# Unread matmuls taken out, two scalings moved from VectorE to GpSimd, and token lists by fp32r products, in a delta-rule attention and mixture-of-experts kernel

## The chip, the cores and the metric

The kernel runs on one core of a Trainium2 chip. The metric is the time of one execution on the device, in microseconds, as the median of several executions. Engines are called by their short names in the profile: PE is the matrix engine, DVE is VectorE, ACT is ScalarE, POOL is GpSimd, and SP is the engine whose queue issues most of the DMA transfers.

## The reference

Two stages follow each other. The first is a linear attention with a delta rule, for 4 batches of 8 heads, 768 positions and 48 channels. The second routes each of the 3072 tokens to one of 8 experts.

```python
for t in range(S):                       # 768 positions
    kt, vt, bt = (k_n[:, :, t], v[:, :, t], beta[:, :, t, None])
    y[:, :, t] = np.einsum('bhd,bhde->bhe', q[:, :, t], state)
    v_old = np.einsum('bhde,bhd->bhe', state, kt)
    state = state + bt[..., None] * np.einsum('bhd,bhe->bhde', kt, vt - v_old)
...
x = y.transpose(0, 2, 1, 3).reshape(3072, 384)
logits = x @ w_gate + modality_bias[modality_id]
e_idx = np.argmax(logits, axis=1)
gate_w = softmax(logits)[np.arange(N), e_idx]
for e in range(8):
    mask = e_idx == e
    out[mask] = gate_w[mask, None] * (np.maximum(x[mask] @ w1[e], 0) @ w2[e])
```

## The kernel before

**The attention.** The 768 positions are cut into 12 chunks of 64, and each chunk into two halves, which gives 24 steps with the index `i`, where `c = i//2` is the chunk. In every step PE makes a handful of small float32 products: `ks` (keys with the state, L416), `y1` and `r` (the chunk's triangular inverse, L380 and L388), `z` (the inverse with the right-hand side, L422), `ds` (the state's update, L428), `qs` and `pz` (the outputs, L436 and L439). DVE and ACT copy the results out of PSUM; `rh` (L418) forms the right-hand side on DVE from the values `vv` and `ks`. Before `rh`, the values of each step are scaled in place by the task `vs` (L393), which multiplies a 128x384 tile. By default `vs` runs on GpSimd; a mark at its place in the order sends it to DVE.

The triangular inverses of the chunks come from a forward substitution for all heads at once (L332 and L333, alternately a multiply and a subtract), in three jobs `J` of four chunks each. Their results go through DRAM: `rd` and `re` store them (L351, L354), and `rl` loads them back in another layout (L371, L374). Loads of keys (`kq`, L153) and values (`kv`, L158), these stores and loads, and the store of outputs (`xd`, L441) all go through SP's one queue, in order.

**The order.** All of the attention's work, the first half of the router and the beginning of the first expert's work are 948 numbered tasks. `ORDER` (L28 to L50) is a list of their numbers, written out by hand; a letter behind a number chooses another engine (`d` is DVE, `g` is GpSimd). `emit` (L495) issues the tasks in this order, and each engine keeps to it strictly. `FILL` (L52) is a second list: `k:n` puts `n` products of the identity with itself (128x128x128, float32) ahead of task `k` (L499). They add into columns of a PSUM bank that nothing reads. Tasks that the prediction names: 557 and 620 are the router products `lg0` and `lg1`, 579 is `z5`, 590 `ks6`, 107 the product `pg4`, 615 `pz7`, 764 `ks17`, 744 the transposes `xt15`, 909 the transposes `xp3` of gathered rows, 866 the transposes `xt23` of the last output tile, 408 and 414 `vs8` and `vs9`, both halves of chunk 4.

**The router and the lists.** Each output tile is transposed (`xt`, L570) and multiplied by the gate weights (`lg`, L575). `part_a` does the ranking for the first 16 tiles, and makes the lists for two units of 512 tokens; it is cut into tasks `pa0` to `pa16` of the order. `part_b` does it for all 24 tiles, after the attention, beside the first expert's work; there and in all later work the order is that of the framework's scheduler. A unit's list says for each of its places which token stands there and with which gate. `lists` (L674) makes it by products: `A` is a one-hot matrix of a token's rank within 128 (L633), and `B` holds, for every block of 128 places, the token's number and its gate where the token belongs to that block, else zero (L690 to L692). Four tiles at a time make a group; the sum over all tiles of `A` transposed with `B` (L698) is the list. In list a, `B` has 2 x 8 columns, in list b 2 x 17.

**The experts.** Each unit gathers its rows (L797, GpSimd's indirect DMA), transposes them (L800), and splits rows and weights into a high and a low part in fp32r, so that three single-pass products give float32 precision (L837 for the first layer, L892 for the second). The result is scaled by the gate (L895) and scattered to the output (L896).

Of the kernel before, what the change touches and what calls it, by code (L numbers as in the profile page):

```python
# [35 lines left out]
68 70 392d 81 396 387d 398 298 537 82 399 299g 546 538 84 400 539 271 548d 86 547 83 85 300 540 311 401 549 541 560 301g 545 562 10 11 552 561 550 302g 551d 564 553d 575 566 303g  # L36
565d 554 555 577 563 556 576 567 304 557 568 305 570 569 306 579 307 558 571 312 572 573 580 578 574 12 313 397 308 309 402 590 581d 359 314 96 585 360 310 582 586 361 592 587 403
13 315 593 583 591 362 99 594 97 595 596d 101 107 98 100 316g 559 584d 317g 600 110 605 318g 601 108 597 602 409 606 111 319g 112 608 598 607 603 599d 14 609 109 320 623 611 588 610
321 589 615 322 604 612 616 414d 618 614 626 323 619 613 620 15 408d 324 621 617 404 625 325g 405 415 624 406 622 638 407 326 627 410 426 639 629 118 411 421 628d 327g 640 412 121 633
119 413 630 634 122 420d 120 123 416 635 328 631 636 427 641 417 637 329 642 632 418 644 330 643 16 653 419 648 655 422 331 649 645 423 433 651 647 654 424 332 652 656 646 17 425  # L40
657 333 668 650 659 129 658 334g 669 670 663 132 660 664 130 428 133 665 661 335 131 134 671 439 429 672 662 432d 430 336 674 673 686 431 18 438 678 687 675 688 679 337 434 680 676
689 19 435 338 681 677 445 436 339 690 437 701 340 692 440 691 702 666 341g 441 696 703 667 442 682 697d 342 698 705 443 450d 704 707 343 693 706 20 444d 711 694 344 708 695 345 683
# [59 lines left out]
class Attention:  # L102
# [35 lines left out]
    def bank(s,n,t): return s.ps.tile([128,512],F32,name=n,tag=t)  # L138

    def plan(s):  # L140
# [318 lines left out]
            add(f"xd{i}","SP",.45,lambda i=i: xd(i),[f"xo{i}"],mb=.2)  # L459
            s.router.tasks(plan,s,i)  # L460

        tp=lambda NH: s.S[0][:,384:384+2*NH].rearrange("q (a b) -> q a b",a=2)
        end=plan.chain("pa",lambda dry: (R.mute() if dry else R).part_a(*(((Mute(),)*3,)+(Mute(),)*4 if dry else (s.places,s.sea,s.prt(),s.mo,tp))),["lt3","y1_17"],prio=900)
        x={}
        def xe(): x["S"]=s.X.slot_of(*s.first)
# [64 lines left out]
class Router:  # L530


    def __init__(s,tc,pc,wg,mod,bias,tok,ident):
        nc=tc.nc; s.tc=tc; s.nc=nc; s.ident=ident; NT=24
        def T(sh,nm,dt=F32): return pc.tile(sh,dt,name=nm)
        s.wg=T([128,3,32],"wg"); mi=T([128,NT,2],"modi",I32); s.tid=T([128,NT],"tid"); bb=T([128,2,8],"mbias")
        s.loads=((s.wg,wg.rearrange("(k p) e -> p k e",p=128)),(mi,mod.bitcast(I32).rearrange("q (t w) -> q t w",w=2)),(bb,bias.rearrange("(o m) e -> o m e",o=1).to_broadcast([128,2,8])),(s.tid,tok))
        s.mi,s.bb=mi,bb
        s.LT=T([128,NT,32],"LT"); s.xt,s.lg,s.le={},{},{}
        s.m=[T([128,NT],f"m{k}") for k in range(2)]; s.L=T([128,NT,8],"L"); s.bt=T([128,NT,8],"btok")  # L540
        G=nc.gpsimd
        s.tri=T([128,128],"tri"); ii=s.tri.bitcast(I32); G.iota(ii,pattern=[[1,128]],base=0,channel_multiplier=0)
        s.iot=T([128,128],"iotf"); G.tensor_copy(s.iot,ii); G.memset(s.tri,1.0)
        G.affine_select(out=s.tri,in_=s.tri,compare_op=ALU.is_gt,fill=0.0,base=0,pattern=[[1,128]],channel_multiplier=-1)
        s.ones=T([128,128],"ones"); G.memset(s.ones,1.0)
        s.keep=T([128,8,NT],"keep"); G.memset(s.keep,1.0); G.memset(s.keep[:,:,0],0.0)
        s.W=T([128,8,NT],"W"); G.memset(s.W,0.0)
        s.zero=T([128,8],"zero8"); G.memset(s.zero,0.0)
        s.em8=T([128,8],"em8"); G.tensor_scalar(s.em8,s.iot[:,0:8],-8.0,None,ALU.add)
        s.edge={512:T([128,6],"edge512"),256:T([128,12],"edge256"),128:T([128,1],"edge128")}  # L550
        G.tensor_scalar(s.edge[512],s.iot[:,1:7],512.0,None,ALU.mult); G.tensor_scalar(s.edge[256],s.iot[:,0:12],256.0,128.0,ALU.mult,ALU.add); G.memset(s.edge[128],0.0)
        s.lo=T([128,NT],"rlo",I32); s.OH=T([128,NT,8],"OH"); s.r=T([128,NT],"rank"); s.gt=T([128,NT],"gtok")
        s.F=T([128,8],"taken"); G.memset(s.F,0.0)

    def load(s,k): s.nc.sync.dma_start(*s.loads[k])
# [28 lines left out]

    def mute(s):
        d=copies.copy(s)
        for n in ("nc","slot","L","LT","bt","em8","ones","tri","W","keep","OH","r","lo","gt","iot","tid","zero","F","edge"): setattr(d,n,Mute())
        return d

    def rank(s,t0,t1,pw,bank):  # L590

        yield "DVE",1.4
        nc=s.nc; V=nc.vector; n=t1-t0; u=f"_{t0}"
        T=lambda sh,nm: pw.tile(sh,F32,name=nm+u,tag=nm,bufs=1)
        Z=s.slot(9 if t0 else 0,"rt"+u)
# [78 lines left out]
    def lists(s,u,t,pi,NH,ids,o0,out,pw,tp,k,zeroed):  # L674
# [2 lines left out]
        nc=s.nc; V=nc.vector; G=getattr(nc,C.lb_e)  # L677
        T=lambda sh,nm,dt=F32: pw.tile(sh,dt,name=nm+u,tag=nm,bufs=1)
        gate,gidx,sidx=(x[:,o0:o0+NH] for x in out)
        if u!="r": V.tensor_scalar(pi,pi,7,None,ALU.arith_shift_right)  # L680
        H=4; AB=[None,None]; ms=[]
        for h in range(0,t+H,H):
            if h<t:
                yield "DVE",.7+3*(.13+H*NH*1e-3)
                if h==0: AB,LB=(s.slot(k+n,f"l{n}"+u) for n in range(2))
                z=slice(512*(h//H%2),512*(h//H%2)+512); A=AB[:,z].rearrange("q (t c) -> q t c",t=H)
                s.onehot(A,h,H)
                B=LB[:,z][:,0:H*2*NH].rearrange("q (h b n) -> q h b n",h=H,b=2)
                bn=lambda a:a[:,h:h+H].unsqueeze(2).to_broadcast([128,H,NH])
                V.tensor_tensor(B[:,:,0],ids.unsqueeze(1).to_broadcast([128,H,NH]),bn(pi),ALU.is_equal)  # L690
                G.tensor_tensor(B[:,:,1],B[:,:,0],bn(s.gt),ALU.mult)
                V.tensor_tensor(B[:,:,0],B[:,:,0],bn(s.tid),ALU.mult)  # L692
                ms.append((h,A,B))
            if h or t==H:
                yield "PE",.5
                g,A,B=ms.pop(0)
                for i in range(H):
                    nc.tensor.matmul(tp.rearrange("q a b -> q (a b)"),A[:,i],B[:,i].rearrange("q a b -> q (a b)"),start=(not zeroed and g+i==0),stop=(zeroed or g+i==t-1),skip_group_check=zeroed)  # L698
        yield "DVE",2.0
        tk=T([128,NH],"tk"); V.tensor_copy(tk,tp[:,0])  # L700
        V.tensor_scalar(gidx,tk,-1.0,0.0,ALU.add,ALU.max)
        V.tensor_copy(gate,tp[:,1])
        a=T([128,NH],"ta",I32); b=T([128,NH],"tb",I32); c=T([128,NH],"tcc",I32); z=T([128,NH],"tz"); f=T([128,NH],"tf"); f2=T([128,NH],"tf2")
        V.tensor_scalar(a,gidx,8,6,ALU.arith_shift_right,ALU.logical_shift_left)
        V.tensor_scalar(b,gidx,63,None,ALU.bitwise_and)
# [26 lines left out]
    def part_b(s,out,sei,sei2,sei3,pw,bank):  # L732
# [255 lines left out]
```

## Time and profile before

| | |
|---|---|
| median of 3 runs | 499.58 us (498.87 to 504.86) |
| the profiled execution | 500.59 us, with a span of 498.9 us |
| mean granted clock of TensorE | 0.97 |
| busy: PE, DVE, ACT, POOL | 463.8, 324.0, 216.4, 118.4 us |
| DMA | 78.22 MB, 157 GB/s on the mean |
| attention, up to the last output tile | about 0 to 259 us |
| list a / list b on PE | 220.9 to 229.1 / 305.8 to 322.5 us |

A row of a timeline gives the start in us, the duration, the engine, the line, the operation with its output and inputs, the number of instructions run together, and in brackets how long the engine stood idle before it and which instruction ended that. A row of the chain gives start, duration and what ran. A row of a table of stretches gives the stretch, its length, the busy time and number of instructions of PE, PE's weight loads, DVE, ACT and POOL, then the granted clock as a share of full speed, the DMA engines' busy share and GB/s. One float32 matmul appears as two records of PE.

### The profile page before, as it was taken

What the parts mean: (1) busy time and instruction counts of PE and PEld (TensorE: products, weight loads), DVE (VectorE), ACT (ScalarE), POOL (GpSimd) and SP (SyncE); (2) the same over time, 40 slices, a digit from 0 to 9 for tenths busy, and PEclk for the clock granted to TensorE, in tenths of its full rate; (3) what the DMA queues carried; (4) which work ended last, traced back from release to release, by engine and by line L of the source; (5) the groups of instructions that cost most, each with busy time, mean ns of one, the idle gap of its engine ahead of it and who ended that gap; (6) DMA issues with size and microseconds to landing.
All of it is one profiled execution on the core that took longest, in us unless ns stands there. A gap on an engine that the chain in (4) does not pass through costs nothing.

```text
span 498.9 us, 15679 instructions
## 1 busy us (share of the span) xinstructions
PE 463.8 (93%) x6589; PEld 423.9 (85%) x6589; DVE 324.0 (65%) x676; ACT 216.4 (43%) x444; POOL 118.4 (24%) x154
## 2 busy tenths in 40 slices
PE   6889999999798979999799999997999999999994
PEld 6779999988698867898678898986898898899993
DVE  2698668889678774787677896525345355347751
ACT  2513467555456752653445433214234334226540
POOL 9011421446032103113311030065022131021111
PEclk8689999999989999998999999998999999999999
DMA  8759105387767877466645544145236326227730
GB/s 268 237 127 251 52 10 148 96 277 236 185 151 209 227 271 196 80 195 188 193 133 157 170 157 129 55 152 206 81 110 204 97 88 197 64 78 239 226 110 22
DMA packets 81328, 78.22 MB, mean 157 GB/s; under 512 B 48041, under 2 KB 71607, under 8 KB 79968
## 3 DMA queue, kind: packets, MB, share of 16 engines
q1 hardware_dynamic: 78048, 67.49, 45.8%
q0 software_dynamic: 3200, 9.64, 5.6%
q8 instruction: 54, 0.88, 0.7%
q14 instruction: 26, 0.21, 0.1%
HBM read 62.42 MB, written 14.88 MB: 155 GB/s over the span
## 4 chain that ended last, share of the span: by engine, by line
PE 71%; DMA 9%; DVE 9%; ACT 4%; issue 4%; SPq 1%; another core or an unknown queue 1%; POOL 0%; POOLq 0%; DVEq 0%; ACTq 0%
PE hpb L837 10%; PE opb L892 9%; PE opa L892 5%; PE gp L181 4%; PE lv L388 3%; PE hpc L837 3%; PE hpa L837 3%; PE opc L892 3%; DMA vv<-in_kv_dram 3%; PE S L499 3%; DMA kqr<-in_kq_dram 2%; PE y L439 2%; PE z L422 2%; PE S L428 2%; PE S L483 2%
## 5 line engine op out<-in xcount | busy, mean ns | idle before, releaser
L892 PE MATMUL opb<-w2hb,h 128*128 128x384 f32 x192 | 52.8, 340 | 0.5 <-DVE oob L895 0.5
L843 DVE SCALAR_TENSOR_TENSOR h<-hpb,h 128x512 fp32r<-128x512 f32 x24 | 16.6, 691 | 43.3 <-ACT h L841 43.3
L837 PE MATMUL hpb<-xh,w1xb 128*128 128x512 f32 x144 | 41.9, 403 | 0.0
L892 PEld LDWEIGHTS opb<-w2hb,h 128*128 128x128 f32 x192 | 34.8, 188 | 1.8 <-DVE oob L895 1.0
L841 ACT ACTIVATE h<-hpb 128x512 fp32r<-128x512 f32 x24 | 14.4, 598 | 50.5 <-PE hpb L837 50.5
L892 PE MATMUL opa<-w2ha,h 128*128 128x384 f32 x128 | 34.3, 342 | 0.6 <-DVE ooa L895 0.6
L892 PE MATMUL opb<-w2lb,h 128*128 128x384 f32 x96 | 32.5, 338 | 0.0
L837 PEld LDWEIGHTS hpb<-xh,w1xb 128*128 128x128 f32 x144 | 27.6, 194 | 4.7
L418 DVE TENSOR_TENSOR RHS<-vv,ks 64x384 f32<-64x384 f32 x44 | 24.2, 550 | 7.4 <-remote 3.7
L332 POOL TENSOR_TENSOR tmx<-T,A 128x456 f32<-128x456 f32 (+10 forms) x20 | 14.2, 710 | 58.1 <-DVE T L333 57.5
L25 ACT COPY Sb<-S 48x192 f32<-48x192 f32 x68 | 21.3, 313 | 13.6 <-PE S L428 7.2
L499 PE MATMUL S<-ident 128*128 128x128 f32 x154 | 25.6, 307 | 1.5 <-DVE Sb L26 0.5
L25 ACT COPY ZT<-z 64x384 f32<-64x384 f32 x36 | 17.0, 472 | 22.6 <-PE z L422 19.6
L499 PEld LDWEIGHTS S<-ident 128*128 128x128 f32 x154 | 21.4, 211 | 3.3 <-issue 0.7
L797 POOL DMA_INDIRECT xgb<-xd,gidxb x12 | 12.5, 1046 | 49.2 <-DVE tf2b L709 24.2
L896 POOL DMA_INDIRECT out_dram<-oob,sidxb x12 | 12.5, 1040 | 49.2 <-DVE oob L895 28.6
L892 PEld LDWEIGHTS opa<-w2ha,h 128*128 128x128 f32 x128 | 23.0, 188 | 1.3 <-DVE ooa L895 0.8
L181 PE MATMUL gp<-kqr 48*64 48x64 f32 x896 | 18.7, 236 | 5.6 <-DMA kqr<-in_kq_dram 3.7
L332 DVE TENSOR_TENSOR tmx<-T,A 128x396 f32<-128x396 f32 (+14 forms) x40 | 21.6, 540 | 2.6 <-POOL T L333 1.8
L422 PE MATMUL z<-RHS,R 128*64 128x96 f32 x384 | 22.0, 256 | 1.2 <-PE gp L181 0.5
L181 PEld LDWEIGHTS gp<-kqr 48*64 48x64 f32 x896 | 16.5, 149 | 7.5 <-DMA kqr<-in_kq_dram 4.3
L416 PE MATMUL ks<-Sb,kqr 112*64 112x96 f32 x352 | 20.3, 250 | 2.5 <-DVE RHS L418 2.2
(348 smaller groups left out, 1195.0 us busy)
## 6 DMA issues: line engine op xcount, KB each, us to landing
kqr<-in_kq_dram SPq DMA_DIRECT2D x10, 1024.0 KB, 5.9
ke<-in_kq_dram SPq DMA_DIRECT2D x10, 512.0 KB, 9.1
vv<-in_kv_dram SPq DMA_DIRECT2D x12, 384.0 KB, 6.5
xd<-xo SPq DMA_DIRECT2D x24, 192.0 KB, 6.3
w1rb<-in_moe_w_dram SPq DMA_DIRECT2D x12, 384.0 KB
w2rb<-in_moe_w_dram SPq DMA_DIRECT2D x12, 384.0 KB, 3.1
kk<-in_kv_dram SPq DMA_DIRECT2D x11, 384.0 KB, 5.0
w1ra<-in_moe_w_dram SPq DMA_DIRECT2D x8, 384.0 KB, 4.8
```

The lines of the kernel that those rows point to most:

```text
L25: if n=="scalar": nc.scalar.copy(o,i)
L181: s.I[f"g{c}"]=mm(t[k][o:o+64,64*(4*g+j):64*(4*g+j)+64],l,s.KQ[c][u:u+48,g,x,1] if a else l,start=True,stop=True)
L332: E[s.e].tensor_tensor(o,T[:,:,lo:lo+na,c:c+1].to_broadcast([128,n,na,nb]),X[:,:,c:c+1,c+1:32].to_broadcast([128,n,na,nb]),ALU.mult)
L388: for h in range(2): x=2*j+h; mm(o[0:64,x],s.YS[i%2][:,x],R[:,x,32:64] if i>7 else w0(s.Wn[i//4],i)[:,4*h+j],start=True,stop=True)
L416: for p in range(2): mm(s.ks[i][64*p:64*p+64,:,j,:],s.KQ[c][:,g,4*p+j,0],hc(s.Sb[g][:,4*p+j,:]),start=True,stop=True)
L418: c,g=divmod(i,2); b=64*p; V.tensor_tensor(s.RHS[g][b:b+64,:,48*p:48*p+48].rearrange("q (h j) c -> q h j c",h=2),s.KV[c,1][b:b+64,g],s.ks[ ...
L422: for h in range(2): mm(s.z[i][64*h:64*h+64,:,j,:],s.R[i%4][:,2*j+h,:],hc(s.RHS[i%2][:,4*h+j,:]),start=True,stop=True)
L499: for _ in range(fill.get(t["k"],0)): s.nc.tensor.matmul(s.S[1][:,384:512],s.ident,s.ident,start=False,stop=True,skip_group_check=True)
L837: if n in ks: mm=s.nc.tensor.matmul(hp[:,v,:],w[:,k,fs],x[:,k,0:T],start=(n==0),stop=(n==8))
L841: if k==0: s.nc.scalar.activation(hh,hp,AF.Relu)
L843: s.nc.vector.scalar_tensor_tensor(hl,hp,0.0,hh.bitcast(F32),ALU.max,ALU.subtract)
L892: mm=nc.tensor.matmul(op,h[:,f%nf,ts_],w[:,f%2,:],start=(n==0),stop=(n==23)); n+=1
```

## The change

- Twenty-one of the 77 unread products go: all of those ahead of tasks 107, 557, 579, 590, 615, 620, 744, 866 and 909, and two of the three ahead of 764.
- Tasks 408 and 414 lose their mark `d`, and so run on GpSimd, at the same places of the order.
- The lists use fp32r operands. The gate is split into a high part (rounded to fp32r) and the rest, and `B` gets four columns for each block instead of two: the token's number, the high gate, the low gate, and the mask they are made from, whose product is not read. The two gate sums are added behind the product. The list for the units beyond the planned ones, `r`, takes two tiles for a group instead of four.

```diff
 ORDER="""...
-... 612 616 414d 618 614 626 323 619 613 620 15 408d 324 621 ...
+... 612 616 414 618 614 626 323 619 613 620 15 408 324 621 ...
...
-FILL="""107:3 114:10 147:6 226:2 248:3 262:2 351:2 353:8 365:2 395:3 406:4 448:2 557:1 579:2 590:4 615:1 620:1 744:1 753:2 764:3 866:5 909:1 913:3 916:2 917:1 924:3"""
+FILL="""114:10 147:6 226:2 248:3 262:2 351:2 353:8 365:2 395:3 406:4 448:2 753:2 764:1 913:3 916:2 917:1 924:3"""
...
+    def split(s,t0,t1):
+        V=s.nc.vector; g,h,l=(x[:,t0:t1] for x in (s.gt,s.gh,s.gl))
+        V.tensor_copy(h.bitcast(F32R),g); V.tensor_tensor(l,g,h,ALU.subtract)
...
+        if u=="a": s.split(0,t)
+        elif u=="b": s.split(0,t)
         if u!="r": V.tensor_scalar(pi,pi,7,None,ALU.arith_shift_right)
-        H=4; AB=[None,None]; ms=[]
+        H=2 if u=="r" else 4; AB=[None,None]; ms=[]
...
-                if h==0: AB,LB=(s.slot(k+n,f"l{n}"+u) for n in range(2))
+                if h==0: AB,LB=(s.slot(k+n,f"l{n}"+u,F32R) for n in range(2))
...
-                B=LB[:,z][:,0:H*2*NH].rearrange("q (h b n) -> q h b n",h=H,b=2)
+                B=LB[:,z][:,0:H*4*NH].rearrange("q (h b n) -> q h b n",h=H,b=4)
                 bn=lambda a:a[:,h:h+H].unsqueeze(2).to_broadcast([128,H,NH])
-                V.tensor_tensor(B[:,:,0],ids.unsqueeze(1).to_broadcast([128,H,NH]),bn(pi),ALU.is_equal)
-                G.tensor_tensor(B[:,:,1],B[:,:,0],bn(s.gt),ALU.mult)
-                V.tensor_tensor(B[:,:,0],B[:,:,0],bn(s.tid),ALU.mult)
+                V.tensor_tensor(B[:,:,3],ids.unsqueeze(1).to_broadcast([128,H,NH]),bn(pi),ALU.is_equal)
+                for x,y in ((1,s.gh),(2,s.gl),(0,s.tid)): G.tensor_tensor(B[:,:,x],B[:,:,3].bitcast(F32),bn(y),ALU.mult)
...
-        V.tensor_copy(gate,tp[:,1])
+        V.tensor_copy(gate,tp[:,1]); V.tensor_tensor(gate,gate,tp[:,2],ALU.add)
```

`G` in `lists` is the engine that the class `C` names as `lb_e`, VectorE before and after.

More of the change, by code (lines that the diff above doesn't have):

```diff
@@ L38 @@
 13 315 593 583 591 362 99 594 97 595 596d 101 107 98 100 316g 559 584d 317g 600 110 605 318g 601 108 597 602 409 606 111 319g 112 608 598 607 603 599d 14 609 109 320 623 611 588 610
-321 589 615 322 604 612 616 414d 618 614 626 323 619 613 620 15 408d 324 621 617 404 625 325g 405 415 624 406 622 638 407 326 627 410 426 639 629 118 411 421 628d 327g 640 412 121 633
+321 589 615 322 604 612 616 414 618 614 626 323 619 613 620 15 408 324 621 617 404 625 325g 405 415 624 406 622 638 407 326 627 410 426 639 629 118 411 421 628d 327g 640 412 121 633
 119 413 630 634 122 420d 120 123 416 635 328 631 636 427 641 417 637 329 642 632 418 644 330 643 16 653 419 648 655 422 331 649 645 423 433 651 647 654 424 332 652 656 646 17 425
@@ L460, in plan @@
             s.router.tasks(plan,s,i)
-        tp=lambda NH: s.S[0][:,384:384+2*NH].rearrange("q (a b) -> q a b",a=2)
+        tp=lambda NH: s.S[0][:,384:384+4*NH].rearrange("q (a b) -> q a b",a=4)
         end=plan.chain("pa",lambda dry: (R.mute() if dry else R).part_a(*(((Mute(),)*3,)+(Mute(),)*4 if dry else (s.places,s.sea,s.prt(),s.mo,tp))),["lt3","y1_17"],prio=900)
@@ L551, in __init__ @@
         G.tensor_scalar(s.edge[512],s.iot[:,1:7],512.0,None,ALU.mult); G.tensor_scalar(s.edge[256],s.iot[:,0:12],256.0,128.0,ALU.mult,ALU.add); G.memset(s.edge[128],0.0)
-        s.lo=T([128,NT],"rlo",I32); s.OH=T([128,NT,8],"OH"); s.r=T([128,NT],"rank"); s.gt=T([128,NT],"gtok")
+        s.lo=T([128,NT],"rlo",I32); s.OH=T([128,NT,8],"OH"); s.r=T([128,NT],"rank"); s.gt,s.gh,s.gl=(T([128,NT],n) for n in ("gtok","ghi","glo"))
         s.F=T([128,8],"taken"); G.memset(s.F,0.0)
@@ L586, in mute @@
         d=copies.copy(s)
-        for n in ("nc","slot","L","LT","bt","em8","ones","tri","W","keep","OH","r","lo","gt","iot","tid","zero","F","edge"): setattr(d,n,Mute())
+        for n in ("nc","slot","L","LT","bt","em8","ones","tri","W","keep","OH","r","lo","gt","iot","tid","gh","gl","zero","F","edge"): setattr(d,n,Mute())
         return d
@@ L679, in lists @@
         gate,gidx,sidx=(x[:,o0:o0+NH] for x in out)
+        if u=="a": s.split(0,t)
+        elif u=="b": s.split(0,t)
         if u!="r": V.tensor_scalar(pi,pi,7,None,ALU.arith_shift_right)
-        H=4; AB=[None,None]; ms=[]
+        H=2 if u=="r" else 4; AB=[None,None]; ms=[]
         for h in range(0,t+H,H):
             if h<t:
-                yield "DVE",.7+3*(.13+H*NH*1e-3)
-                if h==0: AB,LB=(s.slot(k+n,f"l{n}"+u) for n in range(2))
-                z=slice(512*(h//H%2),512*(h//H%2)+512); A=AB[:,z].rearrange("q (t c) -> q t c",t=H)
+                yield "DVE",.7+4*(.13+H*NH*1e-3)
+                if h==0: AB,LB=(s.slot(k+n,f"l{n}"+u,F32R) for n in range(2))
+                z=slice(512*(h//H%2),512*(h//H%2)+512); A=AB[:,z][:,0:128*H].rearrange("q (t c) -> q t c",t=H)
                 s.onehot(A,h,H)
-                B=LB[:,z][:,0:H*2*NH].rearrange("q (h b n) -> q h b n",h=H,b=2)
+                B=LB[:,z][:,0:H*4*NH].rearrange("q (h b n) -> q h b n",h=H,b=4)
                 bn=lambda a:a[:,h:h+H].unsqueeze(2).to_broadcast([128,H,NH])
-                V.tensor_tensor(B[:,:,0],ids.unsqueeze(1).to_broadcast([128,H,NH]),bn(pi),ALU.is_equal)
-                G.tensor_tensor(B[:,:,1],B[:,:,0],bn(s.gt),ALU.mult)
-                V.tensor_tensor(B[:,:,0],B[:,:,0],bn(s.tid),ALU.mult)
+                V.tensor_tensor(B[:,:,3],ids.unsqueeze(1).to_broadcast([128,H,NH]),bn(pi),ALU.is_equal)
+                for x,y in ((1,s.gh),(2,s.gl),(0,s.tid)): G.tensor_tensor(B[:,:,x],B[:,:,3].bitcast(F32),bn(y),ALU.mult)
                 ms.append((h,A,B))
@@ L755, in part_b @@
         s.experts("b",hi,C.SB,sei,pw)
-        s.pib=pi; s.rest=lambda bank: s.lists("r",24,pi,m+NE-s.nm,s.ids[:,s.nm:],s.nm,out,pw,bank[:,0:2*(m+NE-s.nm)].rearrange("q (a b) -> q a b",a=2),6,False)
-        yield from s.lists("b",24,pi,s.nm,s.ids[:,0:s.nm],0,out,pw,bank("tpb")[:,0:2*s.nm].rearrange("q (a b) -> q a b",a=2),6,False)
+        s.pib=pi; s.rest=lambda bank: s.lists("r",24,pi,m+NE-s.nm,s.ids[:,s.nm:],s.nm,out,pw,bank[:,0:4*(m+NE-s.nm)].rearrange("q (a b) -> q a b",a=4),6,False)
+        yield from s.lists("b",24,pi,s.nm,s.ids[:,0:s.nm],0,out,pw,bank("tpb")[:,0:4*s.nm].rearrange("q (a b) -> q a b",a=4),6,False)
         s.experts("c",hi2,NS,sei2,pw)
```

## The prediction

> **What bounds the kernel now.** I read the busy shares first, then the chain of work that ended last, then a table of stretches cut where the chain changes its character, and last the timelines of single engines around each edit.
>
> ```profile
> PE 463.8 (93%) x6589; PEld 423.9 (85%) x6589; DVE 324.0 (65%) x676; ACT 216.4 (43%) x444; POOL 118.4 (24%) x154
> PE 71%; DMA 9%; DVE 9%; ACT 4%; issue 4%; SPq 1%; another core or an unknown queue 1%; POOL 0%; POOLq 0%; DVEq 0%; ACTq 0%
> 130.00:137.20 7.20, 4.54 (x80) 3.73 (x74) 4.24 (x9) 2.67 (x8) 0.98 (x2) 1.00 0.96 275
> 206.50:220.90 14.40, 13.69 (x294) 12.97 (x294) 13.13 (x53) 8.55 (x22) 0.00 (x0) 1.00 0.71 193
> 305.60:322.50 16.90, 16.90 (x104) 15.27 (x103) 10.69 (x24) 4.70 (x8) 0.00 (x0) 1.00 0.16 48
> ```
>
> PE holds 71% of the chain, but that is an average over three regimes. From 305.60 to 322.50, where the second token lists are made, PE is busy all 16.90 us and DVE 10.69: a microsecond off PE there should come off the end. From 206.50 to 220.90, where the first lists are prepared, DVE has 13.13 of 14.40 and PE 13.69: both are near full, so work taken from one and given to the other gains little. From 130.00 to 137.20 neither is full (4.54 and 4.24 of 7.20); a transfer sets the pace. The three parts of the change fall into these three regimes.
>
> **The two value scalings.** Tasks 408 and 414 scale both halves of chunk 4's values. They stand in DVE's stream ahead of the solve's steps and wait there for a load.
>
> ```profile
> 115.14 8.99 DMA RE<-A
> 128.54 4.29 DMA vv<-in_kv_dram
> 132.85 0.56 DVE L393 TENSOR_TENSOR vv<-vv,RR 128x384 f32<-128x384 f32 x1 [3.88 <-DMA vv<-in_kv_dram]
> ...
> 136.03 1.12 DVE L418 TENSOR_TENSOR RHS<-vv,ks 64x384 f32<-64x384 f32 x2
> 137.20 0.88 PE L416 MATMUL ks<-Sb,kqr 112*64 112x96 f32 x16 [2.16 <-DVE RHS L418]
> 113.24 1.67 POOL L393 TENSOR_TENSOR vv<-vv,RR 128x384 f32<-128x384 f32 x2 [6.47 <-DMA vv<-in_kv_dram]
> 135.07 0.73 ACT L25 COPY R<-lv 32x256 f32<-32x256 f32 x2 [1.35 <-PE lv L388]
> ```
>
> DVE stands still 3.88 us until the load lands at 132.83, then does a scaling, a solve step, a scaling, a solve step and only at 136.03 the right-hand side that PE waits for until 137.20. On GpSimd two scalings take 1.67 us: 132.85+1.67=134.52. DVE does its two solve steps ((136.03-132.85-2x0.56)/2 = 1.0 us each) during the wait, so the right-hand side starts at about 134.6 and ends 1.12 later, and PE starts at 135.75 instead of 137.20: 1.45 us. The ScalarE copy that the product behind it needs ends at 135.80, so nothing else is late first. Queued behind the scalings on GpSimd are a solve step (at 136.14 before, now about 134.6) and later another scaling; nobody waits longer. No DMA is issued by the moved steps, and SP's queue is not passed. What is late next is the key load:
>
> ```profile
> 147.48 1.92 SPq L374 DMA_DIRECT2D R<-RD  x4
> 149.50 0.40 SPq L153 DMA_DIRECT2D kqr<-in_kq_dram  x1
> 155.11 1.16 PE L181 MATMUL gp<-kqr 48*64 48x64 f32 x64 [1.28 <-DMA kqr<-in_kq_dram]
> 134.80:138.20 3.40, 1.24 (x29) 1.12 (x29) 2.50 (x7) 0.72 (x2) 1.94 (x2) 1.00 0.81 283
> 138.20:141.60 3.40, 3.40 (x91) 3.28 (x90) 2.71 (x5) 1.22 (x3) 0.00 (x0) 0.50 1.02 320
> 226.90:230.30 3.40, 3.16 (x48) 3.01 (x52) 3.22 (x16) 0.67 (x2) 0.00 (x0) 1.00 0.96 306
> 230.30:233.70 3.40, 3.40 (x66) 2.79 (x60) 1.67 (x5) 0.51 (x2) 1.95 (x2) 0.51 0.78 275
> ```
>
> SP issues it at 149.50, straight behind a block of 1.92 us that starts at 147.48, and PE waits for it at 155.11. SP's queue can move forward only as far as its own blocks allow, so even if PE gains more, about 1.4 us arrives at 155. I take **-1.4 us**; the bounds are 0 (SP doesn't move at all) and -2.4 (the next paragraph's clock loss goes too).
>
> **The clock.** In the stretch 134.80 to 138.20 PE worked 1.24 of 3.40 us, and in the next the granted clock was 0.50. A second such pair is at 226.90 and 230.30. With PE starting 1.45 us earlier the first stretch holds about 2.7 us of work, and the half-clock stretch may vanish: worth 1.0 by the eighteen products shown with the rivals. SP's limit swallows this, so I count it at nothing. The Trainium skill, "TensorE: Matmul & The Clock Gate", section "Part 1: The HAM clock gate", says that the array's clock is halved after a window of about 3.4 us without enough activity, which speaks against taking unread matmuls out. The first pair agrees; the second does not by busy time, since PE showed 3.16 of 3.40 before it. That rule is a rival below.
>
> **The unread matmuls.** 77 become 56, and each is two records:
>
> ```profile
> L499 PE MATMUL S<-ident 128*128 128x128 f32 x154 | 25.6, 307 | 1.5 <-DVE Sb L26 0.5
> 192.43 0.91 PE L499 MATMUL S<-ident 128*128 128x128 f32 x6 [0.51 <-DVE Sb L26]
> ...
> 194.07 0.49 PE L499 MATMUL S<-ident 128*128 128x128 f32 x2
> 256.68 1.12 PE S L499 x10
> 255.98 0.56 DVE L26 COPY xo<-y 128x384 f32<-128x384 f32 x1 [0.26 <-PE y L439]
> ```
>
> There are 154 records, and the old fill list sums to 77, the new one to 56: 21 go. Ten records take 1.12 us on the chain: 0.22 us for a matmul. Twelve of them stand, by the written order, between the first router product and the second, 108 to 132 us. There the chain runs through the solve's end, the store that takes 8.99 us from 115.14, SP and the load from 128.54; PE is not in it. Their 2.6 us go into PE's waiting: 0 taken (bounds 0 to -0.6, if the key load that precedes that store in SP's queue leaves earlier by the three that stand before it). At 192.43 two of three go and at 194.07 the only one: 3 x 0.22 = **-0.6 us**, PE being the bound from there to 198. At 256 all six go. The five at 256.68 cover the copy of the last output tile, 255.98 to 256.54, which the following transposes need; those could start at 256.6 instead of 257.80: **-1.1 us**, with PE full behind it. Bounds 0 and -1.3.
>
> **The lists.** A float32 product is two records, and a single-pass product should be one:
>
> ```profile
> 305.81 1.71 PE tpb L698 x16
> 227.14 2.00 PE S L698 x16
> 263.31 0.66 PE xpa L800 x6
> 456.26 2.13 PE hpc L837 x18
> 222.63 0.82 DVE L690 TENSOR_TENSOR l1a<-iotf,pia 128x32 f32<-128x32 f32 x1
> 223.49 0.76 DVE L691 TENSOR_TENSOR l1a<-l1a,gtok 128x32 f32<-128x32 f32 x1
> 224.28 1.20 DVE L692 TENSOR_TENSOR l1a<-l1a,tid 128x32 f32<-128x32 f32 x1
> 227.84 0.19 DVE L692 TENSOR_TENSOR l1a<-l1a,tid 128x32 f32<-128x32 f32 x1
> ...
> 316.08 0.22 DVE L691 TENSOR_TENSOR l1b<-l1b,gtok 128x68 f32<-128x68 f32 x1
> ...
> 222.12 2.07 POOL L393 TENSOR_TENSOR vv<-vv,RR 128x384 f32<-128x384 f32 x2 [18.70 <-DVE ZT L26]
> 224.16 1.26 POOL L197 TENSOR_TENSOR pb<-pb,cst 128x512 f32<-128x512 f32 x1
> ```
>
> In list b eight products (16 records) take 1.71 us, 0.214 each, and there are three such groups. No single-pass product with 68 columns is in the trace. The nearest rows are the one-record transposes, 128 columns in 0.66/6 = 0.11 us, and fp32r with 256 columns, 2.13/18 = 0.118. I take 0.11, the transposes being nearer in width: 24 x (0.214-0.11) = **-2.5 us**. The bounds are -2.3 and, were it to cost only its share of columns (0.118 x 68/256 = 0.03), -4.4; nothing at all if what follows waits for something else. DVE gains one multiply of 0.22 for each of six groups, and two split operations and an addition that I price like it at most, under 2.0 us in all, in a stretch where it has 6.2 free: 0.
>
> In list a sixteen products take 0.25 each (2.00/8), 4.0 in all, and would lose about 2.2. But there DVE has no room: four more multiplies (0.19 each), two split operations and an addition, priced alike, 1.3 us, of which about 0.5 fits into a wait of DVE ahead of the third group. The last group was ready at 228.03 and would be ready at about 228.7; its four products then end at 229.2, against 229.14 before. So the PE saving turns into a wait for DVE: 0 taken, bounds +1.2 and -2.2. Where GpSimd ran at 222.12 and 224.16, three operations of 0.19 on DVE took 0.82, 0.76 and 1.20; the fourth multiply may fall there too, which is in the upper bound.
>
> **The sum.** -1.4-0.6-1.1-2.5 = -5.6 us on the profiled execution, whose time is 500.59 (span 498.9 and 1.7 around it): 495.0. That execution lies 1.0 above the median of 499.58, so the forecast for a median is **494.0**.
>
> **Rivals.**
>
> *More than summed.* Both half-clock stretches vanish and list a is freed, because everything ahead of it starts earlier: -1.0 (SP's queue moves along), -1.0 and -2.2 on top: 489.8. For it: the stretches follow low PE load, which shrinks. Against it: DVE's 13.13 of 14.40. Chance 0.13.
>
> *Hidden anyway.* The scaling's gain is swallowed at 155 and list b's at the gather behind it, leaving -0.6 and -1.1: 497.9. For it: at 155.11 PE does wait for a load. Chance 0.17.
>
> *Clock.* The fills gone, PE's load drops and more half-clock stretches come. One costs 1.0:
>
> ```profile
> 286.65 0.62 PE L892 MATMUL opa<-w2ha,h 128*128 128x384 f32 x2 [0.56 <-DVE ooa L895]
> 335.93 2.33 ACT L824 CAST w2hb<-w2rb 128x768 fp32r<-128x768 f32 x3 [4.54 <-PE xpb L800]
> 340.01 0.90 PE L800 MATMUL xpb<-ident,xgb 128*128 128x128 f32 x3 [4.34 <-DVE xl L803]
> 340.91 5.18 PE hpb L837 x18
> 377.04 4.17 PE hpb L837 x18
> ```
>
> (18 products in 5.18 against 4.17.) Four on the path make it 498.0. Chance 0.12. By the skill's rule named above this is what removed activity brings.
>
> *Slower.* Part b's instructions are ordered by the scheduler, not by the written order, and new ones among them can turn the order at a unit boundary. At 340.01 PE waits 4.34 us because three casts, 2.33 us from 335.93, stand in ScalarE's queue ahead of the copies that free the transposes' buffers, and then loses 1.0 to the clock. One more such boundary, at the first expert's end near 286, costs 5.3 and makes list b's saving worthless, as PE would wait behind it: 499.6-1.4-0.6-1.1+5.3 = 501.8. It decides as soon as a list operation delays the first unit's last conversions by more than the 0.56 us that PE waits there now. Chance 0.10.
>
> *Not single-pass.* If the new product takes two records, list b gives nothing: 496.5. Chance 0.03. That leaves 0.45 for the forecast, 491.5 to 497.
>
> **Range.** The lower end, 489.5, takes in part of the first rival and the bounds of list b; the upper, 500.0, all but the slower one. A measurement of this kernel tells about 2% from no change, 10 us: below 489.6 I see 0.08, above 509.6 only 0.02, and between 0.90.
>
> **What would show it.** In the changed profile the two scalings stand on GpSimd near 133, the right-hand side begins near 134.6, and the product at 137.20 starts 1.4 earlier; the granted clock of the stretch behind it tells of the second bound. Fills between 108 and 132 missing without a shift of the load at 128.54 show that they were free. The transposes after 256.6 follow directly. Each group of list b takes 0.9 us with eight records. List a ends within 0.3 us of its old place counted from its first preparation, with PE idle before the last group. The forecast is wrong if new idle stands on PE after 260, if the load at 155.11 doesn't move, or if a list product takes less than 0.08 or more than 0.15.

## The result, and the profile after

The changed kernel takes 495.32 us (median of 21 runs) where the kernel before takes 499.58 (21 runs). The medians differ by 4.3 us, but every ratio here is taken over the means without the slow executions that both kernels have now and then, and that ratio is 0.9929, 95% interval 0.9901 to 0.9957: -3.5 us, between -4.9 and -2.1. The forecast was 494.0. A second measurement (run five below) gave 0.9930 (0.9902 to 0.9959). The profiled execution has a span of 493.3 us.

From the page of the changed kernel, the busy shares and the chain; then two rows of its table of stretches, in the columns of the table shown for before:

```profile
PE 457.1 (93%) x6507; PEld 416.0 (84%) x6507; DVE 324.4 (66%) x690; ACT 215.8 (44%) x444; POOL 122.0 (25%) x156
PE 69%; DVE 11%; DMA 10%; issue 4%; ACT 4%; SPq 1%; POOL 0%; another core or an unknown queue 0%; POOLq 0%; DVEq 0%; ACTq 0%
...
130.00:137.20 7.20, 7.20 (x130) 6.09 (x128) 6.03 (x11) 4.65 (x14) 3.82 (x4) 1.00 0.88 234
305.60:322.50 16.90, 16.54 (x91) 15.01 (x90) 9.48 (x33) 3.64 (x6) 2.58 (x3) 1.00 0.30 87
```

PE does 6.7 us less work and the span is 5.6 shorter. Those rows can't simply be set against before's, because single executions of one kernel differ by several microseconds (494.2 to 504.9 for the kernel before). I therefore count from an instruction ahead of every edit, the right-hand side near 103 us: at 103.23 before, at 104.75 after.

**What the early unread products did.** Rows of the timelines of PE, DVE, ScalarE and SP's queue, first before, then after:

```profile
103.23 1.12 DVE L418 TENSOR_TENSOR RHS<-vv,ks 64x384 f32<-64x384 f32 x2 [1.25 <-PE ks L416]
108.17 0.49 PE L499 MATMUL S<-ident 128*128 128x128 f32 x2
112.12 0.88 PE L436 MATMUL y<-Sb,kqr 112*64 112x96 f32 x16
112.61 2.02 ACT L348 COPY A<-T 64x1024 f32<-64x1024 f32 x1
113.05 0.33 SPq L153 DMA_DIRECT2D kqr<-in_kq_dram  x1
115.14 1.79 SPq L354 DMA_DIRECT2D RE<-A  x2
```

```profile
104.75 1.12 DVE L418 TENSOR_TENSOR RHS<-vv,ks 64x384 f32<-64x384 f32 x2 [1.25 <-PE ks L416]
109.69 0.86 PE L575 MATMUL lg<-xs,wg 128*32 128x128 f32 x24
112.43 0.88 PE L436 MATMUL y<-Sb,kqr 112*64 112x96 f32 x16
112.91 1.97 ACT L348 COPY A<-T 64x1024 f32<-64x1024 f32 x1
113.35 0.33 SPq L153 DMA_DIRECT2D kqr<-in_kq_dram  x1
114.91 2.27 SPq L354 DMA_DIRECT2D RE<-A  x2
```

The key load in SP's queue leaves right behind the product at 112.12, which reads the keys' old buffer. Counted from the mark, that product starts at 8.89 before and at 7.68 after, the key load at 9.82 and 8.60, the store behind it in the same queue at 11.91 and 10.16. So PE stands in this chain, through the buffer. It stands there a second time, through ScalarE. The store writes what ScalarE's copies (L348) make, and ScalarE reaches them only behind its copies of PE's results. The first of them ends 11.40 behind the mark before (112.61+2.02) and 10.13 after (112.91+1.97). Before, the store leaves half a microsecond later than that, as the issues ahead of it in SP's queue end (115.04); after, it leaves 0.03 behind the copy. In the other traces, run ten's apart, it is the same: with the products in, the queue releases the store, with them out, the copy. Had only the key load come earlier, the store could not have left before 11.40.

Three unread products stood ahead of the product at 112.12. From the first of them to that product are 3.95 us (112.12-108.17); after, from the router product that stands first now, 2.74 (112.43-109.69). So the three had cost 0.40 each, not 0.22.

The prediction named the load of values at 128.54 as the sign: if it did not shift, the products were free. It left 25.31 behind the mark before and leaves 22.97 after (127.72). As a sign it is not clean, since in run three below it leaves at 21.65 with the products in.

**What the scalings did.** After, timelines of GpSimd, DVE and PE:

```profile
133.30 2.37 POOL L393 TENSOR_TENSOR vv<-vv,RR 128x384 f32<-128x384 f32 x2 [7.24 <-ACT xs L25]
135.71 1.11 DVE L418 TENSOR_TENSOR RHS<-vv,ks 64x384 f32<-64x384 f32 x2 [0.73 <-POOL vv L393]
142.09 1.21 POOL L393 TENSOR_TENSOR vv<-vv,RR 128x384 f32<-128x384 f32 x1 [4.46 <-DMA vv<-in_kv_dram]
154.73 1.16 PE L181 MATMUL gp<-kqr 48*64 48x64 f32 x64 [1.05 <-DMA kqr<-in_kq_dram]
```

The right-hand side starts 2.41 us behind the first scaling, against 3.18 before (136.03-132.85). It would have been about 1.7 had the two scalings taken the 1.67 that the prediction took from GpSimd's row; they took 2.37. PE no longer waits there (it is busy all of 130.00 to 137.20, in the rows above). But at 154.73 it waits for the same key load as before.

**What the late unread products did.** First the ones at 192 and 194 us: a row of PE before, then two of after.

```profile
197.04 1.12 PE L388 MATMUL lv<-R,YS 128*64 128x32 f32 x16
```

```profile
189.72 0.46 PE L499 MATMUL S<-ident 128*128 128x128 f32 x2 [0.50 <-DVE Sb L26]
193.62 1.12 PE L388 MATMUL lv<-R,YS 128*64 128x32 f32 x16
```

From the unread products (192.43 before, in the prediction's rows) to the inverse's product are 4.61 us before and 3.90 after: 0.7 for the three that went. Over the same stretch the other traces without them gain 0.3 to 0.7 too. Then the last output tile, a row of before and the rows of after:

```profile
257.88 0.94 PE L837 MATMUL hp<-xh,w1xa 128*128 128x512 f32 x3
```

```profile
252.18 0.56 DVE L26 COPY xo<-y 128x384 f32<-128x384 f32 x1 [0.26 <-PE y L439]
252.79 0.55 PE L570 MATMUL rxt<-ident,xo 128*128 128x128 f32 x3 [0.18 <-DVE xo L26]
253.16 0.56 DVE L808 TENSOR_TENSOR xl<-xp,xh 128x384 fp32r<-128x384 f32 x1 [0.42 <-ACT xh L807]
253.77 0.96 PE L842 MATMUL hp<-xh,w1xa 128*128 128x512 f32 x3 [0.43 <-DVE xl L808]
```

The transposes do follow their copy directly. But the first layer's products behind them now wait for the conversion of the gathered rows, which DVE does only behind ScalarE's. From the copy's start to those products are 1.90 us before (257.88-255.98) and 1.59 after: 0.3 of the 1.1 that was forecast. Every trace without these products has the 1.59.

### The profile page after: what moved, and what is told of

Read it like the earlier page. It is cut to its first block, busy times and chain, and to the rows that moved or that the text cites. A ratio compares the mean times of both kernels' runs of the same rounds, so it can differ in the third digit from the quotient of the medians.

```text
span 493.3 us, 15531 instructions
## 1 busy us (share of the span) xinstructions
PE 457.1 (93%) x6507; PEld 416.0 (84%) x6507; DVE 324.4 (66%) x690; ACT 215.8 (44%) x444; POOL 122.0 (25%) x156
## 4 chain that ended last, share of the span: by engine, by line
PE 69%; DVE 11%; DMA 10%; issue 4%; ACT 4%; SPq 1%; POOL 0%; another core or an unknown queue 0%; POOLq 0%; DVEq 0%; ACTq 0%
PE hpb L842 10%; PE opb L897 9%; PE opa L897 5%; PE gp L181 4%; DMA kqr<-in_kq_dram 4%; PE lv L388 3%; PE hpc L842 3%; PE opc L897 3%; PE hpa L842 3%; DMA vv<-in_kv_dram 3%; PE S L428 2%; PE S L499 2%; PE y L439 2%; PE z L422 2%; PE S L483 2%
## 5 line engine op out<-in xcount | busy, mean ns | idle before, releaser
L439 PE MATMUL y<-ZT,pb 128*64 128x96 f32 x384 | 22.3, 258 | 1.1 <-DVE ZT L26 1.1
L333 DVE TENSOR_TENSOR T<-T,tmx 128x396 f32<-128x396 f32 (+14 forms) x40 | 21.7, 543 | 1.4
L422 PEld LDWEIGHTS z<-RHS,R 128*64 128x64 f32 x384 | 17.7, 138 | 5.2 <-DVE pb L192 2.4
L897 PE MATMUL opa<-w2la,h 128*128 128x384 f32 x64 | 21.8, 341 | 0.0
```

What stands on the lines that cost most here:

```text
L333: x=T[:,:,lo:lo+na,c+1:32]; E[s.e].tensor_tensor(x,x,o,ALU.subtract)
L422: for h in range(2): mm(s.z[i][64*h:64*h+64,:,j,:],s.R[i%4][:,2*j+h,:],hc(s.RHS[i%2][:,4*h+j,:]),start=True,stop=True)
L439: for p in range(2): mm(s.y[i][64*p:64*p+64,:,j,:],s.PB[i//2][:,8*(i%2)+4*p+j],hc(s.ZT[i%2][:,4*p+j,:]),start=(i<2 and j==0),stop=True,ski ...
L897: mm=nc.tensor.matmul(op,h[:,f%nf,ts_],w[:,f%2,:],start=(n==0),stop=(n==23)); n+=1
```

## The experiments

Each was timed beside the kernel before, which took 490.4 to 501.4 us on the chips used. Ratios are to it, with 95% intervals.

**One: the 21 unread products alone.**

```diff
-FILL="""107:3 114:10 ... 924:3"""
+FILL="""114:10 147:6 ... 924:3"""   (the changed kernel's list; all else as before)
```

> The kernel before, with only the 21 unread products taken out. Theory of the sum: -1.7 us against before (-0.6 at 192 to 194 us, -1.1 at 256 us, nothing for the twelve at 108 to 132 us). Rival, the clock: the missing activity brings further half-clock stretches, each worth about +1.0 us where it lies on the path, so between -0.7 and +1. Rival, queue: the key load ahead of the store leaves earlier, another -0.6, -2.3 in all. In the profile the sum wants the load of vv at 128.54 unmoved and the last output transposes directly behind their copy.

Measured: 0.9916 (0.9880 to 0.9953), -4.1 us (-5.9 to -2.3), more than the sum's -1.7; the -2.3 of the queue rival lies at the interval's edge. The key load leaves 8.60 us behind the mark, as that rival has it.

**Two: the scalings alone.** `414d` and `408d` become `414` and `408`.

> The kernel before, with only tasks 408 and 414 moved to GpSimd. Theory of the sum: -1.4 us against before, the right-hand side 1.4 earlier and the wait for the key load at 155 earlier by the same. Rival, hidden: the gain ends at the wait for the key load at 155, 0 us. Rival, clock goes with it: the half-clock stretch at 138 vanishes, -2.4.

Measured: 0.9996 (0.9964 to 1.0028). Its timelines:

```profile
133.30 1.63 POOL L393 TENSOR_TENSOR vv<-vv,RR 128x384 f32<-128x384 f32 x2 [7.30 <-DMA vv<-in_kv_dram]
134.96 1.12 DVE L418 TENSOR_TENSOR RHS<-vv,ks 64x384 f32<-64x384 f32 x2 [2.46 <-POOL vv L393]
143.61 0.65 DVE L332 TENSOR_TENSOR tmx<-T,A 128x468 f32<-128x468 f32 x1 [2.03 <-POOL T L333]
155.84 1.16 PE L181 MATMUL gp<-kqr 48*64 48x64 f32 x64 [3.88 <-DMA kqr<-in_kq_dram]
```

Here the scalings take 0.82 each and the right-hand side follows the first by 1.66 instead of 3.18 us: the 1.5 that was forecast is there. It is gone at 155.84, where PE waits 3.88 us for the key load. Counted from the mark that is 51.25, and 51.47 to 51.88 in before and in runs three, eight and nine, which have the scalings on VectorE. This is the rival "Hidden anyway", for this part.

**Three: the lists alone.** The changed kernel with the old order marks and the old list of unread products.

> The kernel before, with only the lists by single-pass fp32r products. Theory of the sum: -2.5 us against before, all of it behind 300 us; list a ends at its old place within 0.3 us. Rival, list a freed too: -4.7, with list a's end about 2.2 earlier. Rival, hidden: 0, because a gather or a copy behind list b sets the pace. Rival, slower: a unit boundary with a new wait of some 5 us, +2.8.

Measured: 0.9922 (0.9890 to 0.9954), -3.8 us.

**Four: the twelve early unread products put back** into the changed kernel (`107:3 557:1 579:2 590:4 615:1 620:1`).

> The changed kernel, with the twelve unread products ahead of tasks 107, 557, 579, 590, 615 and 620 (108 to 132 us) put back. Theory of the sum: the same time as the changed kernel, since PE waits there anyway. Rival, clock: the half-clock stretch that the changed kernel's trace shows at 122.8 us goes, and the time falls by up to 1.0 us against the changed kernel. Rival, on the path: +2.6 us against the changed kernel (twelve at 0.22).

Measured: 0.9962 (0.9927 to 0.9996), some 0.3% slower than the changed kernel against the same kernel before, with overlapping intervals. That is about 1.6 us, between the sum's nothing and the 2.6 of the rival "on the path". The clock rival's gain of 1.0 did not come.

**Five: the changed kernel again**, beside the next three.

> The changed kernel unaltered, beside its parts on one chip. If the parts' effects add (fills alone 0.9916 and lists alone 0.9922 of before on a first chip, scalings alone 0.9996), 0.983, some -8 us. If the parts share a gain, or if the three together cost something that no part costs alone, about 0.993, -3.5 us, as in its first measurement.

Measured: 0.9930 (0.9902 to 0.9959). The parts' effects don't add.

**Six: the changed kernel without the moved scalings.** `414` and `408` get their `d` back.

> The changed kernel with tasks 408 and 414 back on VectorE: fills and lists without the scalings. If the scalings are worth nothing (their gain ends at the key load at 155 us), the same as the changed kernel. Theory of the sum: 1.4 us slower than the changed kernel. Rival: the scalings slow GpSimd or VectorE elsewhere, and this one is 2 to 4 us faster than the changed kernel.

Measured: 0.9932 (0.9898 to 0.9966), the same as five: no worth of the scalings is seen. By times alone neither this run nor run two excludes -1.4; the traces below do better.

**Seven and eight: the early twelve and the late nine alone.**

```diff
+FILL="""114:10 ... 448:2 744:1 753:2 764:3 866:5 909:1 913:3 ..."""   (seven: the early ones out)
+FILL="""107:3 114:10 ... 557:1 579:2 590:4 615:1 620:1 753:2 764:1 913:3 ..."""   (eight: the late ones out)
```

> The kernel before without the twelve unread products at 108 to 132 us alone. Prediction's sum: 0. Queue theory, from the traces with them out: the key load at 113.05 and the store behind it in SP's queue leave 1.2 to 1.7 us earlier, and with them all that waits for that store, so -1.2 to -1.7 us, unless the wait at 155 us swallows it.

> The kernel before without the nine unread products at 192, 194 and 256 us alone. Prediction's sum: -0.6 -1.1 = -1.7 us. From the traces with them out the transposes' part at 256 us is -0.3 instead of -1.1, which makes -0.9. Rival: the gain ends at VectorE's full stretch at 206 to 221 us, -0.3.

Measured: seven 0.9939 (0.9905 to 0.9973), -3.0 us; eight 0.9987 (0.9953 to 1.0021), -0.6 us. Rows of seven:

```profile
105.06 1.12 DVE L418 TENSOR_TENSOR RHS<-vv,ks 64x384 f32<-64x384 f32 x2 [1.26 <-PE ks L416]
113.66 0.33 SPq L153 DMA_DIRECT2D kqr<-in_kq_dram  x1
115.24 2.26 SPq L354 DMA_DIRECT2D RE<-A  x2
```

Key load at 8.60 and store at 10.18 from the mark. The prediction's "0 taken" for the early twelve is wrong; for the late nine, -1.7 is not excluded, but the point lies at a third of it.

**The eight traces together.** All in us, the first three columns from the mark near 103, the others between two instructions of one trace (chunk 6's key products to the first expert's first layer; that to the end; list b's first product to the next unit's first layer):

| run | early products | key load | store | chunk 6's key products | to first layer | to the end | list b to next unit |
|---|---|---|---|---|---|---|---|
| two | in | 9.81 | 12.12 | 51.25 | 97.8 | 237.3 | 30.83 |
| three | in | 9.81 | 12.65 | 51.49 | 96.5 | 233.9 | 28.97 |
| four | in | 9.81 | 12.34 | 52.88 | 96.2 | 234.2 | 28.99 |
| eight | in | 9.81 | 12.04 | 51.54 | 97.2 | 235.5 | 30.81 |
| one | out | 8.60 | 10.18 | 49.64 | 97.9 | 236.5 | 30.81 |
| five | out | 8.60 | 10.14 | 50.92 | 97.2 | 233.9 | 28.97 |
| six | out | 8.60 | 10.15 | 50.64 | 96.5 | 233.5 | 28.96 |
| seven | out | 8.60 | 10.18 | 50.54 | 96.1 | 235.2 | 30.83 |

The early products: 51.8 on the mean with them, 50.4 without, -1.4 us. The traces of before and of run nine (in: 51.88 and 51.47) and the first of the changed kernel (out: 49.98) fall in line. The scalings make no such difference: with them on GpSimd (two, four, five) 51.25, 52.88 and 50.92, on VectorE 51.49 and 51.54 with the early products in, 49.64, 50.64 and 50.54 with them out. The new lists (three to six): 233.9 to the end against 236.1, -2.3. The middle stretch as a whole is too uneven to show the late products' 0.7 and 0.3 (out in one, four, five, six, eight). The early products and the lists together make -3.7, close to the whole change's -3.4 to -3.5. The times of the parts alone, -4.1, -0.2 and -3.8, add to -8.1 with an uncertainty of some 3; whether that excess is chance or a gain that fills and lists share, the runs don't settle. The -1.4 counted for the early products lies just inside the interval of run seven (-4.7 to -1.3).

**Nine: list a alone.** The kernel before with the fp32r form for list a, list b as before.

> The kernel before, with only list a by single-pass fp32r products; list b keeps its old form. Prediction's sum: 0, because VectorE's fourth multiplication takes what the products give. Rival, list a freed: about -2.2 us; the traces with both new lists show the stretch from its first product to its last at 6.4 or 7.5 us instead of 8.2, so -0.8 to -1.8 us there, and the key load behind it (waited for at about 231 us) may take that back: 0. If nearly all of the lists' -3.8 us came from list a, list b would be worth less than -1.85 us, the amount by which the traces shorten the stretch from list b to the next unit's first layer.

Measured: 0.9987 (0.9955 to 1.0019), -0.6 us (-2.2 to +1.0). The prediction's 0 is not contradicted, but its reason holds only in part. From the changed kernel's timelines of GpSimd, DVE and PE:

```profile
218.21 1.90 POOL L393 TENSOR_TENSOR vv<-vv,RR 128x384 f32<-128x384 f32 x2 [18.70 <-DVE ZT L26]
219.40 0.76 DVE L697 TENSOR_TENSOR l1a<-l1a,ghi 128x32 fp32r<-128x32 f32 x1
220.08 1.31 DVE L697 TENSOR_TENSOR l1a<-l1a,glo 128x32 fp32r<-128x32 f32 x1
223.83 0.19 DVE L697 TENSOR_TENSOR l1a<-l1a,tid 128x32 fp32r<-128x32 f32 x1
224.08 0.62 PE L703 MATMUL S<-l1a,l0a 128*128 128x32 f32 x4 [0.90 <-DVE l1a L697]
```

PE's last four products take 0.62 us and wait 0.90 for DVE's last multiplication, at 223.83; two of the multiplications took 0.76 and 1.31 instead of 0.19 while GpSimd multiplied (its scalings, and another behind them to 221.34). So DVE now sets the pace there. But it doesn't take all that PE saves: from DVE's operation that makes the tokens' places for list a (`pia`, L727 before, L732 after) to the end of the list's last product are 13.6 to 13.8 us in every trace with the old form and 11.9 to 13.5 with the new one, the split operations included. It is 12.97 in the trace of the rows above, 12.72 in run nine, and 11.90 in run six, where no multiplication was slowed. The prediction had it unchanged within 0.3. What becomes of this gain behind the list was not traced.

**Ten: no unread products at all** in the changed kernel.

> The changed kernel with the other 56 unread products taken out as well. If unread products only cost their PE time where PE is the bound: faster than the changed kernel, by anything up to 56 x 0.22 = 12 us, likely 2 to 4 since most stand in waits of PE. Clock rival: the missing activity brings more half-clock stretches (the changed kernel has four between 100 and 345 us in its first trace), each about +1 us, and this one is slower than the changed kernel by 1 us for each new one on the path.

Measured: 0.9935 (0.9908 to 0.9962), the same as the changed kernel. PE has 9.8 us less work (447.3 busy), but pays in clock: the mean granted clock is 0.951 in the median of its executions, against 0.967 for the kernel before beside it. Two rows of its table of stretches:

```profile
91.80:95.20 3.40, 2.48 (x38) 2.33 (x40) 3.30 (x7) 1.12 (x4) 1.63 (x2) 0.64 0.02 5
95.20:98.60 3.40, 3.40 (x90) 3.22 (x84) 1.56 (x3) 0.40 (x2) 1.84 (x2) 0.50 0.02 5
```

The clock stays at half to some 106 us, in a place where no other trace has it. So the clock rival is real for products that this change leaves in place; what it costs in time was not separated.

**Eleven: chunk 6's keys one block earlier in SP's queue**, in the changed kernel.

```diff
-... 328 631 636 427 641 417 637 ... 330 643 16 653 ...
+... 328 631 636 641 16 427 417 637 ... 330 643 653 ...
```

Task 16 is the load; the edit also brings task 641 ahead of 427.

> The changed kernel with the load of chunk 6's keys one block earlier in SP's queue (ahead of the loads of step 12's inverse, instead of behind them). If that load is what takes the scalings' gain back: it leaves at about 146 instead of 149.6 us, PE's wait of 1 to 2 us at 155 us goes, and the time falls by 1 to 2 us against the changed kernel. Rival, next in line: the loads of the inverse, 0.5 to 1.2 us later now, become the new wait at 157 us, and nothing is gained.

Measured: 0.9884 (0.9851 to 0.9917), -5.8 us, against -3.5 for the changed kernel; the fastest of all that ran, though its interval overlaps the changed kernel's. Its timelines:

```profile
145.07 0.38 SPq L153 DMA_DIRECT2D kqr<-in_kq_dram  x1
152.24 1.16 PE L181 MATMUL gp<-kqr 48*64 48x64 f32 x64
```

The wait for the keys is gone: 152.24 lies 49.39 behind the mark, against 50.92 in run five and 49.98 in the changed kernel's first trace. So the trace shows a gain of 0.6 to 1.5 us, and the rest of the 2.3 between the two measured times is not traced.

**Twelve: the same, with the scalings back on VectorE.**

> The changed kernel with the load of chunk 6's keys one block earlier, as in the run before, and tasks 408 and 414 back on VectorE. If the key load was what took the scalings' gain back, the scalings count here: PE's products of chunk 6's keys start some 1.2 to 1.5 us later after the first scaling than the 20.5 us with the scalings on GpSimd, about 21.9, and the time rises by about 1.4 us, to 0.991 of before. Rival: the scalings are worth nothing in any case, since VectorE makes up for them before 150 us; then 20.5 us and 0.988.

Measured: 0.9923 (0.9894 to 0.9953). The time rose by 0.4%, as in the first theory, with overlapping intervals; but the trace doesn't show it. There the products of chunk 6's keys start 19.4 us behind the first scaling, earlier than eleven's 20.5. So the rise isn't the scalings' where they were looked for, and whether they are worth anything beside an earlier key load stays open. What stands between, in before (DVE), in five (DVE) and in twelve (GpSimd, PE):

```profile
144.80 0.65 DVE L332 TENSOR_TENSOR tmx<-T,A 128x468 f32<-128x468 f32 x1 [0.97 <-POOL T L333]
```

```profile
144.99 0.65 DVE L332 TENSOR_TENSOR tmx<-T,A 128x468 f32<-128x468 f32 x1 [2.83 <-POOL T L333]
```

```profile
140.13 0.83 POOL L393 TENSOR_TENSOR vv<-vv,RR 128x384 f32<-128x384 f32 x1 [2.27 <-DVE ZT L26]
151.94 1.16 PE L181 MATMUL gp<-kqr 48*64 48x64 f32 x64
```

In five DVE stands 2.83 us for a solve step on GpSimd, which is queued behind the next scaling (at 142.09 in the changed kernel's rows above, where it waits for the next load of values). The longer wait alone doesn't tell of the moved scalings: it is 0.97 in before and in twelve, but 2.84 in run six, all with the scalings on VectorE. What tells is the order: in all fourteen traces DVE's step starts 3.2 to 3.3 us behind GpSimd's next scaling, wherever the first two ran. On the mean it starts 40.6 behind the mark with those on GpSimd and 40.7 with them on VectorE (run ten apart). So the load of values sets that step, and what DVE gains at 134 us is gone there, ahead of the key load. In twelve that load came early enough for the scaling to start at 140.13. A gain made behind one load is lost at the next.

## Why the prediction was right or wrong

**The whole** came out inside the range and the forecast's own 491.5 to 497, at 495.3; the measured -3.5 is smaller than the summed -5.6. That it lies so near is in part luck: the -1.4 of the scalings did not come, and a -1.4 that was not in the sum came from the early products. What the traces show term by term is 0 for the scalings, -1.4 for the early products, -0.7 and -0.3 for the late ones and -1.85 for list b, together some -4.2, inside the measured -4.9 to -2.1.

**The scalings, -1.4: wrong.** The local step was right (1.5 us in run two). The step that failed is "even if PE gains more, about 1.4 us arrives at 155", an assumption about SP's queue; no gain is seen to arrive (run two 0.9996; run six the same as five; no earlier start of chunk 6's key products in the traces). What the prediction left out stands ahead of 155: at 144 us DVE needs a step of GpSimd that is queued behind the next load of values, and it starts there no earlier with the scalings moved (40.6 against 40.7 behind the mark).

**The early products, 0: wrong.** "PE is not in it" was the failing step. PE is in the chain, through the key buffer that SP waits for and through the copies that ScalarE makes behind PE's results. The bound of -0.6 named this path, with three products ahead of it, but at 0.22 each; the trace shows 1.2 us for the three at the key load, and -1.4 at chunk 6's keys.

**The late products, -0.6 and -1.1: the first right, the second oversized.** Run eight gives -0.6 for both (-2.3 to +1.0), which excludes neither. The traces give 0.7 for the three at 192 us and 0.3 for the six at 256. There the transposes follow directly, as forecast, but "with PE full behind it" failed: PE waits 0.43 us for the conversion at 253.16.

**List b, -2.5: right in mechanism, oversized.** The product is single-pass. From the chains of runs seven (old) and five (new), and PE's timeline of each at the next unit:

```profile
299.22 1.71 PE tpb L698 x16
329.59 0.55 PE L800 MATMUL xpb<-ident,xgb 128*128 128x128 f32 x3 [0.50 <-DVE xl L803]
```

```profile
300.07 0.82 PE tpb L703 x8
307.45 0.37 PE tpb L703 x4
328.88 1.66 PE L842 MATMUL hpb<-xh,w1xb 128*128 128x512 f32 x6 [0.84 <-ACT xh L807]
```

Three groups of 1.71 became one of 0.82 and four of 0.37: 5.13 against 2.30, that is 0.10 a product where 0.11 was taken, and -2.8 on PE. Of that -1.85 arrives at the next unit's first layer (the table's last column, where the four traces of each form agree within 0.03). In the new form PE waits 0.84 us there for ScalarE's conversion, and 0.36 at 318.01 for DVE's scaling of a result (L900); in the old form its only wait in the stretch is the 0.50 for DVE's conversion. That accounts for 0.7 of the missing 1.0; where the rest goes was not traced.

**List a, 0: not contradicted by the time (0.9987 alone), but the reason is half wrong.** The wait of 0.90 for DVE ahead of the last group is there. "So the PE saving turns into a wait for DVE" is the step that failed: in the traces the list ends 0.1 to 1.9 us earlier, counted from `pia`, and by more than the prediction's own sign of 0.3 in all but run five.

**The clock, 0: not contradicted.** The stretch that ran at half clock behind 138 us in before is gone, and a new one has come near 120. Before, then after:

```profile
119.40:122.80 3.40, 3.40 (x107) 3.09 (x104) 2.99 (x7) 0.47 (x1) 2.95 (x8) 1.00 0.97 384
122.80:126.20 3.40, 3.32 (x67) 2.85 (x65) 2.83 (x7) 1.10 (x3) 1.60 (x3) 1.00 0.19 54
```

```profile
119.40:122.80 3.40, 1.19 (x28) 0.88 (x26) 2.36 (x5) 0.20 (x2) 3.19 (x6) 0.99 1.02 403
122.80:126.20 3.40, 3.40 (x84) 3.28 (x86) 2.77 (x6) 0.47 (x1) 2.87 (x6) 0.50 0.24 64
```

Without the early products PE works 1.19 of the 3.40 us ahead of it. This held in the traces of the changed kernel and of runs one, five, six, seven, eleven and twelve (a half-clock stretch near 120 us), while before and runs two, three, four, eight and nine have theirs at 137 to 158 us instead. The Trainium skill, "TensorE: Matmul & The Clock Gate", section "Part 1: The HAM clock gate", has the clock halved after an idle window of about 3.4 us. These rows agree in direction only, because the stretch ahead of the halving is not idle but shows 1.19 us of work. Near here, taking activity out moved the halving rather than adding one. Over the whole middle it is less clear: between 100 and 345 us before has three halvings, and the changed kernel four in its first trace and two in run five's, one of them twice as long. Run four, which has no halving near 120, shows no gain of 1.0 from it.

## What to carry to other kernels

A DMA queue that runs in order makes an engine critical through the buffer that the next load overwrites: before an engine's wait is called free, look at which of its products releases the head of that queue, and which of them the copies wait for that a store in it needs. A gain made between two waits for loads is worth only what the next load gives back, so follow it there before it enters a sum. Where effects are below 1% and executions scatter by as much, count each trace from a common instruction ahead of the edits: steps came out equal to 0.03 us there that the medians could not separate.

## What the runs showed of the hardware that was not expected

An unread float32 product between other products cost 0.40 us, against 0.22 in a row of five. An fp32r product with 68 columns takes 0.09 to 0.10 us.

Some of list a's multiplications on DVE took 0.7 to 1.3 us instead of 0.19. In all 17 such cases, from all traces, the multiplication ended 0.04 to 0.05 us behind the end of a multiplication on GpSimd. In the changed kernel's rows these are 220.16 behind 220.11 and 221.39 behind 221.34.

At the second unit's boundary some chips show a stall that others don't. In the changed kernel's first trace, ScalarE and PE:

```profile
331.41 2.30 ACT L829 CAST w2hb<-w2rb 128x768 fp32r<-128x768 f32 x3 [3.12 <-PE xpb L805]
334.52 2.93 PE L842 MATMUL hpb<-xh,w1xb 128*128 128x512 f32 x6 [4.55 <-ACT xh L807]
```

ScalarE stands still for 3.12 us. The row names PE's transposes as what ended it, but those had been done for 1.4 us; a cause is not visible. PE waits 4.55. The same instructions wait 0.84 us in run five, which is the same kernel. Before, after and runs nine to eleven have the stall (PE waits 4.06 to 4.55 us); runs one to eight and twelve don't. Nine to eleven ran on one chip, the others on three more; for before and after the chip isn't recorded. The median of the kernel before differed by some 10 us between these groups. The prediction's rival "Slower" was built on this stall as if the order of the instructions made it; the same order runs without it elsewhere. Its cause is open.
